# Attention scores from one full pass and one pass of half the rows, with two blocks of keys side by side

## The chip, the cores and the metric

The kernel runs on one core of a Trainium2 chip. The metric is the device time of one execution in microseconds (us); lower is better. The engines are named as the profile names them: PE is the matrix engine, PEld its loads of the stationary operand, DVE, ACT and POOL the vector, scalar and general engines, and SP the queue that issues most transfers.

## What is computed

The reference, cut to its three parts, with 8 batches of 3072 rows, 256 columns and 64 score dimensions:

```
scores = matmul(z, z.T) / S                  # per batch, z is 3072 x 64
x = u * matmul(maximum(scores, 0) ** 2, v)   # attention without a softmax
x = x / sqrt(mean(x * x) + 1e-6) * rms_g     # norm over the 256 columns
x = (silu(x @ w_gate) * (x @ w_val)) @ w_out
out = for each row: the expert with the largest x @ r_gate, relu(x @ w1[e]) @ w2[e], times two gates
```

All is kept close to float32 by cutting each operand into a high and a low part of the type float32r and summing the products high by high, high by low and low by high.

## The kernel before

**Tiling.** A batch's 3072 rows are 6 groups of 512 queries, J counts these 48 groups, and 24 blocks of 128 keys, taken two at a time. So a group has 12 steps, counted by `kp`, and there are 576 such steps of attention (class `Attn`). 18 steps behind them (`AHEAD`) runs the gated layer of the group (class `Glu`), 12 steps of its own per group, one for each 128 of the 1536 hidden columns. The function `pair` writes one step of each, interleaved by hand; the order on each engine is the order of writing. The experts follow when both are done.

**Operands of the scores.** `z_job` transposes 512 rows of z into a tile `p`: partitions 0 to 63 hold the high part of z transposed (64 dimensions), partitions 64 to 127 the low part, for every block of keys. The low part is DVE's line L441, the high part ACT's line L450. `make_q` copies `p` of the group's own 512 queries with the halves exchanged into a tile `q`, by two ACT instructions (L468, L471) that stand two steps apart. In `Attn.first` each block of keys takes two passes over 512 queries with the same stationary slice of `p`: L504 streams `p` (high by high plus low by low), L505 streams `q` (high by low plus low by high), and both sum in one PSUM bank `s`. ACT's L507 reads the bank (relu and scale), L512 squares, L515 rounds to the high part `ha`, DVE's L521 makes the low part `la`, and one step later L535 to L537 multiply them by v, 24 passes of 256 columns.

**Order of PE in a step.** Scores of this step (4 passes of 512), gate and value products of the gated layer (L648, 12 passes of 512), products with v of the step before (24 of 256), output product of the gated layer of the step before (L673 to L675, 6 of 512). PSUM has four banks for scores and gate products together (pool `sc`), handed out in turn.

**Around a group.** `load_u` fetches the group's u (512 KB) in the middle of the group, at `kp` 6; the tile has one buffer. `Attn.leave` multiplies the sums by u into a tile `x`, squares it on ACT into u's tile for the norm's sums (L552), scales x (L568) and turns it by 16 DVE blocks into `xf` (L599). These stand in `side`, a planner that gives out queued work step by step and is forced (`side.until`) where a result is needed. `split_x` then rounds `xf` on ACT (L628) and DVE (L629) to `xTh` and `xTl`, on which the next group's first L648 waits. `f32t("sg")` has two buffers, for the gate products `sg`. SP works in order; each of its transfers is written behind those that were written before it.

**Parts of the array's rows.** An operand of up to 32 or up to 64 partitions is set by the built program on a quarter or a half of the array's 128 rows. Before, only four instructions are: the transposes of a 12-row table (L894) in the first of two calls of `table`; those of the second call have 91 rows and stand on all 128.

Of the kernel before, what the change touches and what calls it, by code (L numbers as in the profile page):

```python
# [8 lines left out]
F32 = mybir.dt.float32  # L9
F32R = mybir.dt.float32r  # L10
# [3 lines left out]
AF = mybir.ActivationFunctionType  # L14
ALU = mybir.AluOpType
# [10 lines left out]
def attention_glu_routed(ctx: ExitStack, tc: tile.TileContext, u, v, z, w_gate, w_val, w_out, rms_g, r_gate, r_og, w1, w2, out):  # L26
# [12 lines left out]
    nc = tc.nc  # L39
    B, S, D = u.shape  # L40
    DQ = z.shape[2]
    FF = w_gate.shape[1]
    E, _, F2 = w1.shape
# [23 lines left out]
    sc = ctx.enter_context(tc.tile_pool(name="sc", bufs=4, space=PSUM))  # L67
# [7 lines left out]
    def bank(pool, name):  # L75
        return pool.tile([128, 512], F32, tag="sc" if pool is sc else "acc", name=name)
# [3 lines left out]
    def f32t(tag, name):  # L80
        return st.tile([128, 512], F32, tag=tag, name=name, bufs=BUFS.get(tag, 2))
# [318 lines left out]

    vt, pt, qt = {}, {}, {}
    z_chain = Chain()

    def v_job(b, kp, tag):
        t = {}
# [15 lines left out]
    def z_job(b, c, tag):  # L421
        t = {}

        def load():
            t["r"] = f32t(tag, "z_raw")
            nc.sync.dma_start(
                out=t["r"][:, 0:256].rearrange("p (a d) -> p a d", a=4), in_=z[b, c * 512 : (c + 1) * 512, :].rearrange("(a p) d -> p a d", p=128)
            )

        def work():  # L430
            z_chain.end()
            zf = bank(sc, "zT")
            for i in range(2):
                nc.tensor.transpose(zf[:, i * 128 : (i + 1) * 128], t["r"][:, i * 128 : (i + 1) * 128], ident)
            x = at.tile([128, 512], F32R, tag="p", name="p", bufs=NC)
            xv = x.rearrange("p (i k c) -> p i k c", i=2, k=2)
            zv = zf[:, 0:256].rearrange("p (i c) -> p i c", i=2)

            def low():
                for k in range(2):  # L440
                    nc.vector.tensor_tensor(  # L441
                        out=xv[64:128, :, k], in0=zv[64 * k : 64 * k + 64], in1=xv[0:64, :, k].bitcast(F32), op=ALU.subtract
                    )
                pt[b, c] = x
                if c == 0:
                    make_q(b * NC)

            def high():
                for k in range(2):
                    nc.scalar.activation(out=xv[0:64, :, k], in_=zv[64 * k : 64 * k + 64], func=AF.Copy)  # L450

            z_chain.begin(high, low)

        return load, 0.6, work, tag, 3.9 if b else 0.0
# [8 lines left out]

    def make_q(J):
        b, c = divmod(J, NC)
        q = at.tile([128, 512], F32R, tag="q", name="q")
        p = pt[b, c]
        nc.scalar.activation(out=q[0:64], in_=p[64:128].bitcast(F32), func=AF.Copy)  # L468

        def other():  # L470
            nc.scalar.activation(out=q[64:128], in_=p[0:64].bitcast(F32), func=AF.Copy)  # L471
            qt[J] = q

        if J:
            side.after(2, other)
        else:
            other()


    xt, xf, ut = {}, {}, {}  # L480
    squared, turned = set(), set()

    def load_u(J):
        b, c = divmod(J, NC)
# [3 lines left out]
    class Attn:  # L488
# [7 lines left out]
        def first(self):  # L496
            b = self.b
            ahead = min(NC - 1, (self.kp + 2) // 2)
            side.until(lambda: (b, ahead) in pt and self.J in qt and (b, 2 * max(0, self.kp - 1)) in vt, -1)
            for j in range(2):  # L500
                kb = 2 * self.kp + j
                ps = bank(sc, "s")
                w = pt[b, kb // 4][:, (kb % 4) * 128 : (kb % 4 + 1) * 128]
                nc.tensor.matmul(ps, lhsT=w, rhs=pt[b, self.c], start=True, stop=False)  # L504
                nc.tensor.matmul(ps, lhsT=w, rhs=qt[self.J], start=False, stop=True)  # L505
                r = f32t("r", "r")
                nc.scalar.activation(out=r, in_=ps, func=AF.Relu, scale=SCALE)  # L507
                self.r.append(r)
# [30 lines left out]
        def leave(self):  # L539
            J = self.J  # L540
            side.until(lambda: J == 0 or J - 1 in turned, 0)
            x, uu = at.tile([128, 4, D], F32, tag="x", name="x", bufs=1), ut.pop(J)
            xt[J] = x
            for k in range(2):
                v4 = lambda t: t[:, 2 * k : 2 * k + 2]
                nc.vector.tensor_tensor(out=v4(x), in0=self.accs[k].rearrange("p (a c) -> p a c", a=2), in1=v4(uu), op=ALU.mult)
            ss, y, tmp = small([128, 4], "ss"), small([128, 4], "yi", I32), small([128, 4], "nt")
            yf = y.bitcast(F32)

            def squares(k):  # L550
                for qb in (2 * k, 2 * k + 1):
                    nc.scalar.activation(out=uu[:, qb], in_=x[:, qb], func=AF.Square, accum_out=ss[:, qb : qb + 1])  # L552
                if k:
                    squared.add(J)

            def root():

                nc.vector.tensor_scalar(out=ss, in0=ss, scalar1=1.0 / D, scalar2=1e-6, op0=ALU.mult, op1=ALU.add)
                nc.vector.tensor_scalar(out=y, in0=ss.bitcast(I32), scalar1=-0.5, scalar2=1597463007.0, op0=ALU.mult, op1=ALU.add)
                for _ in range(3):  # L560
                    nc.gpsimd.tensor_tensor(out=tmp, in0=yf, in1=yf, op=ALU.mult)
                    nc.gpsimd.tensor_tensor(out=tmp, in0=tmp, in1=ss, op=ALU.mult)
                    nc.gpsimd.tensor_scalar(out=tmp, in0=tmp, scalar1=-0.5, scalar2=1.5, op0=ALU.mult, op1=ALU.add)
                    nc.gpsimd.tensor_tensor(out=yf, in0=yf, in1=tmp, op=ALU.mult)

            def scale(k):
                for qb in (2 * k, 2 * k + 1):
                    nc.scalar.activation(out=x[:, qb], in_=x[:, qb], func=AF.Copy, scale=yf[:, qb : qb + 1])  # L568

            side.add(1.0, None, 0)  # L570
            side.add(0.1, lambda: squares(0), 0)
            side.add(0.1, lambda: squares(1), 0)
            side.add(3.0, None, 0)
            side.add(0.4, root, 0)
            side.add(6.0, None, 0)
            side.add(0.1, lambda: scale(0), 0)
            side.add(0.1, lambda: scale(1), 0)
            side.add(2.0, None, 0)
            turn_x(J)
# [497 lines left out]
    def pair(n, m):  # L1077

        a = g = None
        if n is not None:  # L1080
            J, kp = divmod(n, NP)
            a = Attn(J, kp, lists.setdefault(("a", J), []))
            a.first()
        if m is not None:
            J, f = divmod(m, NF)
            side.until(lambda: J in xT, 0)
            g = Glu(J, f, lists.setdefault(("g", J), []))
            g.first()
        pa, pg = last["a"], last["g"]
        last["a"], last["g"] = a, g  # L1090
        for step in (pa, pg):
            if step:
                step.second()
        if a:
            a.high(0, nc.scalar if g else nc.vector)
        t = Turn()
        t.time = (3.75 if a else 0.0) + (4.19 if g else 0.0)
        t.budget = 4.0 if a and g else 1.5 if a else 1.9
        side.tick(t)
        if a:  # L1100
            a.low(0)
        if g:
            g.gate()
            g.product()
            if g.f == NF - 1 and g.J + 1 < NJ - 1:
                side.until(lambda: g.J + 1 in turned, 0)
                split_x(g.J + 1)
        if a:
            a.high(1, nc.scalar if g else nc.vector)
            a.low(1)  # L1110
        if g:
            g.part()
            g.rest()
        if pa and pa.kp == NP - 1:
            pa.leave()
        if pg and pg.f == NF - 1 and pg.J < NJ - 1:
            pg.leave()
        if a:

            if a.kp == NP // 2 and a.J:  # L1120
                side.until(lambda: a.J - 1 in squared, 0)
                load_u(a.J)
            if a.kp == NP // 2 and a.c < NC - 1:
                make_q(a.J + 1)
            if a.c == NC - 1 and a.b + 1 < B:
                if a.kp % 2:
                    side.jobs([z_job(a.b + 1, a.kp // 2, "raw")])
                if a.kp:
                    side.jobs([v_job(a.b + 1, a.kp - 1, "raw")])
            if a.c == 0 and a.b and a.kp == 0:  # L1130
                side.jobs([v_job(a.b, NP - 1, "raw")])
            if a.J >= 2 and a.kp in (NP // 2, NP - 1):
                spare(1)
# [98 lines left out]
```

## Time and profile before

| | us |
|---|---|
| median of 3 runs | 6101.07 (6096.69 to 6106.18) |
| the profiled execution | 6110.35 |
| its span, first to last instruction | 6108.6 |
| PE busy | 5868.4 (96%) |
| DVE busy | 4141.2 (68%) |
| ACT busy | 3418.4 (56%) |
| mean granted clock of PE | 0.983 |

A row of a timeline gives start and duration in us, engine, line, operation, the tile written and the tiles read; brackets give the idle time before it and what ended it. The ends of matmuls are modelled and overlap the next start, so the pace of PE is read from start to start. A PEld row is the load of the stationary slice for the matmul of the same line; in a steady stream it starts together with the matmul before.

### The profile page before, as it was taken

Reading aid. Unit: us, or ns where it says so; the run is one execution under the profiler, and the core shown is the slowest. Engines: PE = TensorE matmul, PEld = TensorE weight load, DVE = VectorE, ACT = ScalarE, POOL = GpSimd, SP = SyncE. Lnnn points to the kernel's source line nnn. Section 1 sums busy time; section 2 is a strip of 40 time slices with the busy share of each in tenths; the row PEclk is TensorE's granted clock in tenths of the full one; section 3 lists DMA queues with packets and bytes.
Section 4 is the critical chain, followed back from the end, with each engine's and each line's share of the span. In section 5 each row is a group of like instructions: output and inputs, shape, how many; then the busy total and the mean of one; then the engine's idle time right before and its main releaser. Section 6 shows DMA issues by size and latency. Waiting matters only on the chain. (4 is left out here: it accounts for less than half of the span.)

```text
span 6108.6 us, 95345 instructions
## 1 busy us (share of the span) xinstructions
PE 5868.4 (96%) x35032; PEld 5155.5 (84%) x35032; DVE 4141.2 (68%) x8920; ACT 3418.4 (56%) x6610; POOL 1151.3 (19%) x1729
## 2 busy tenths in 40 slices
PE   6899999999999999999999999999999889999998
PEld 5688888888888888888888888888888779999998
DVE  6666666665666566666666666657565678888886
ACT  4566666666666666666666666666666423333332
POOL 2212101210121012101211030103000023333333
PEclk8999999999999999999999999999999999999999
DMA  2101100110010001001110010001000112232241
GB/s 70 47 25 49 34 25 30 46 34 23 30 49 30 23 30 49 30 27 32 47 32 22 29 32 13 15 12 36 8 15 8 47 55 101 101 103 101 102 139 57
DMA packets 199592, 268.27 MB, mean 44 GB/s; under 512 B 46988, under 2 KB 176016, under 8 KB 190928
## 3 DMA queue, kind: packets, MB, share of 16 engines
q1 hardware_dynamic: 173664, 210.29, 10.7%
q0 software_dynamic: 25456, 51.83, 2.7%
q8 instruction: 278, 4.55, 0.3%
q14 instruction: 194, 1.59, 0.1%
HBM read 528.71 MB, written 86.71 MB: 101 GB/s over the span
## 5 line engine op out<-in xcount | busy, mean ns | idle before, releaser
L537 PE MATMUL o<-v,la 128*128 128x256 f32 x4608 | 1298.3, 282 | 29.3 <-DVE la L521 29.2
L535 PE MATMUL o<-v,ha 128*128 128x256 f32 x4608 | 1291.9, 280 | 5.3 <-DVE ha L517 5.2
L536 PE MATMUL o<-v,ha 128*128 128x256 f32 x4608 | 1291.2, 280 | 0.0
L521 DVE TENSOR_TENSOR la<-r,ha 128x512 fp32r<-128x512 f32 x1152 | 835.9, 726 | 663.5 <-ACT ha L515 658.0
L507 ACT ACTIVATE r<-s 128x512 f32<-128x512 f32 x1152 | 624.8, 593 | 859.4 <-PE s L505 806.5
L648 PE MATMUL g<-xTh,wg 128*128 128x512 f32 x2304 | 844.7, 408 | 131.9 <-ACT xTh L628 102.7
L656 DVE TENSOR_TENSOR sg<-g,sg 128x512 f32<-128x512 f32 x1152 | 793.9, 689 | 196.0 <-ACT sg L652 133.5
L537 PEld LDWEIGHTS o<-v,la 128*128 128x128 f32 x4608 | 871.5, 189 | 33.2 <-DVE la L521 32.9
L535 PEld LDWEIGHTS o<-v,ha 128*128 128x128 f32 x4608 | 872.6, 189 | 29.5 <-DVE ha L517 6.4
L536 PEld LDWEIGHTS o<-v,ha 128*128 128x128 f32 x4608 | 871.9, 189 | 25.6
L648 PE MATMUL g<-xTh,wv 128*128 128x512 f32 x2304 | 831.2, 402 | 5.7 <-ACT wv L93 3.0
L515 ACT ACTIVATE ha<-r 128x512 fp32r<-128x512 f32 x1116 | 705.7, 632 | 38.6
L512 ACT ACTIVATE r<-r 128x512 f32<-128x512 f32 x1152 | 721.7, 627 | 1.0
L648 PEld LDWEIGHTS g<-xTh,wg 128*128 128x128 f32 x2304 | 443.2, 192 | 263.7 <-ACT xTh L628 122.9
L1007 PE MATMUL h<-gh,W 128*128 128x256 f32 x3200 | 641.2, 283 | 5.4 <-ACT gh L93 4.1
L660 ACT ACTIVATE hg<-sg 128x512 fp32r<-128x512 f32 x576 | 363.6, 631 | 487.2 <-DVE sg L656 431.3
L1026 PE MATMUL eo<-W,hx 128*128 128x512 f32 x1600 | 580.2, 395 | 0.7 <-DVE o L1039 0.7
L1007 PEld LDWEIGHTS h<-gh,W 128*128 128x128 f32 x3200 | 526.9, 191 | 25.3 <-ACT gh L93 5.5
L648 PEld LDWEIGHTS g<-xTh,wv 128*128 128x128 f32 x2304 | 446.1, 194 | 109.9 <-PE g L648 3.8
L599 DVE STREAM_TRANSPOSE gTf<-xg 32x128 f32<-32x128 f32 x1600 | 483.3, 302 | 49.2 <-DMA xg<-xs,clip 26.9
L1010 ACT ACTIVATE hx<-h 128x512 fp32r<-128x512 f32 x400 | 236.7, 595 | 496.0 <-PE h L1007 493.5
L96 POOL TENSOR_TENSOR le<-e_raw,he 128x512 fp32r<-128x512 f32 x64 | 83.0, 1297 | 2119.9 <-ACT he L93 2119.9
(170 smaller groups left out, 11046.8 us busy)
## 6 DMA issues: line engine op xcount, KB each, us to landing
W<-ws SPq DMA_DIRECT2D x400, 1024.0 KB
v_raw<-in_v SPq DMA_DIRECT2D x96, 256.0 KB
u<-in_u SPq DMA_DIRECT2D x48, 512.0 KB
xs<-rec SPq DMA_DIRECT2D x48, 512.0 KB
e_raw<-in_moe_w SPq DMA_DIRECT2D x64, 256.0 KB
ws<-he SPq DMA_DIRECT2D x64, 256.0 KB
ws<-le SPq DMA_DIRECT2D x64, 256.0 KB
z_raw<-in_z SPq DMA_DIRECT2D x48, 128.0 KB
```

The lines of the kernel that those rows point to most:

```text
L507: nc.scalar.activation(out=r, in_=ps, func=AF.Relu, scale=SCALE)
L512: nc.scalar.activation(out=r, in_=r, func=AF.Square)
L515: nc.scalar.activation(out=self.ab[j][0], in_=r, func=AF.Copy)
L521: nc.vector.tensor_tensor(out=l, in0=self.r[j], in1=h.bitcast(F32), op=ALU.subtract)
L535: nc.tensor.matmul(o, lhsT=ah[:, cs], rhs=vh, start=kb == 0 and qb % 2 == 0, stop=False, skip_group_check=True)
L536: nc.tensor.matmul(o, lhsT=ah[:, cs], rhs=vl, start=False, stop=False, skip_group_check=True)
L537: nc.tensor.matmul(o, lhsT=al[:, cs], rhs=vh, start=False, stop=kb == NK - 1, skip_group_check=True)
L599: nc.vector.transpose(out=ov[32 * q : 32 * q + 32, :, :, i, :], in_=iv[32 * i : 32 * i + 32, :, :, q, :])
L648: nc.tensor.matmul(ps, lhsT=a[:, d, fs], rhs=x[:, d], start=n == 0, stop=n == 5)
L656: nc.vector.tensor_tensor(out=self.sg, in0=ps, in1=self.sg, op=ALU.mult)
L1007: nc.tensor.matmul(o, lhsT=w[:, c0 : c0 + 128], rhs=x[:, d], start=n == 0, stop=n == 5)
L1026: nc.tensor.matmul(self.accs[t], lhsT=h[:, cs], rhs=w, start=f == 0, stop=False)
```

## The change

Three things are changed.

First, the scores. `p` now holds, for even blocks of keys, the high part in partitions 0 to 63 and the low part in 64 to 127, and for odd blocks the other way round. There are two query tiles: `q0` has the high part in both halves, `q1` the low part in both. A step first streams `q0` through all 128 rows for both blocks (L503: high by high plus low by high), then streams one half of `q1` for each block through that half of the rows that holds the keys' high part (L506: high by low), rows 0 to 63 for the even block and 64 to 127 for the odd one. The product low by low is no longer computed. Both PSUM banks of a step are taken ahead of the first matmul, and the two relu instructions stand behind all four matmuls.

Second, `make_q` is eight transfers inside SBUF on SP (64 partitions by 2 by 128 numbers each) in place of two ACT instructions.

Third, to pay for the second query tile, the tile `x` is gone: u is overwritten by the norm's input, the squares go to a buffer of `sg`, and `load_u` of a group waits until the group before is turned, where it waited for its squares.

```
@@ z_job: low and high
-                        out=xv[64:128, :, k], in0=zv[64 * k : 64 * k + 64], in1=xv[0:64, :, k].bitcast(F32), op=ALU.subtract
+                    here, there = half[k], half[1 - k]
+                    nc.vector.tensor_tensor(out=xv[there, :, k], in0=zv[here], in1=xv[here, :, k].bitcast(F32), op=ALU.subtract)
-                    nc.scalar.activation(out=xv[0:64, :, k], in_=zv[64 * k : 64 * k + 64], func=AF.Copy)
+                    nc.scalar.activation(out=xv[half[k], :, k], in_=zv[half[k]], func=AF.Copy)
@@ make_q
-        q = at.tile([128, 512], F32R, tag="q", name="q")
-        nc.scalar.activation(out=q[0:64], in_=p[64:128].bitcast(F32), func=AF.Copy)
...
-            nc.scalar.activation(out=q[64:128], in_=p[0:64].bitcast(F32), func=AF.Copy)
+        qs = [at.tile([128, 512], F32R, tag=f"q{k}", name=f"q{k}") for k in range(2)]
+        for part in range(2):
+            for k in range(2):
+                for to in half:
+                    nc.sync.dma_start(out=view(qs[part])[to, :, k].bitcast(F32), in_=view(pt[b, c])[half[k ^ part], :, k].bitcast(F32))
@@ Attn.first
-            for j in range(2):
-                kb = 2 * self.kp + j
-                ps = bank(sc, "s")
-                w = pt[b, kb // 4][:, (kb % 4) * 128 : (kb % 4 + 1) * 128]
-                nc.tensor.matmul(ps, lhsT=w, rhs=pt[b, self.c], start=True, stop=False)
-                nc.tensor.matmul(ps, lhsT=w, rhs=qt[self.J], start=False, stop=True)
+            pss = [bank(sc, "s") for _ in kbs]
+            for ps, w in zip(pss, ws):
+                nc.tensor.matmul(ps, lhsT=w, rhs=qh, start=True, stop=False)
+            for ps, w, h in zip(pss, ws, half):
+                nc.tensor.matmul(ps, lhsT=w[h], rhs=ql[h], start=False, stop=True)
+            for ps in pss:
                 r = f32t("r", "r")
                 nc.scalar.activation(out=r, in_=ps, func=AF.Relu, scale=SCALE)
@@ Attn.leave
-            x, uu = at.tile([128, 4, D], F32, tag="x", name="x", bufs=1), ut.pop(J)
+            x = xt[J] = ut.pop(J)
-                    nc.scalar.activation(out=uu[:, qb], in_=x[:, qb], func=AF.Square, accum_out=ss[:, qb : qb + 1])
+                t = f32t("sg", "xx")
+                    nc.scalar.activation(out=t[:, i * D : (i + 1) * D], in_=x[:, qb], func=AF.Square, accum_out=ss[:, qb : qb + 1])
@@ pair
-                side.until(lambda: a.J - 1 in squared, 0)
+                side.until(lambda: a.J - 1 in turned, 0)
                 load_u(a.J)
```

On PE, in a step of attention with the gated layer beside it, the rows stood so before; `y` is the output product of the step before, `s` the scores (tiles `p` and `q`), `g` the gate products:

```order
L675 MATMUL y_5768<-hg_6372,wo1_99 128x512
L504 MATMUL s_6492<-p_5371,p_5572 128x512
L505 MATMUL s_6492<-q_5565,p_5572 128x512
L504 MATMUL s_6497<-p_5371,p_5572 128x512
L505 MATMUL s_6497<-q_5565,p_5572 128x512
L648 MATMUL g_6502<-xTh_5601,wg0_94 128x512
L648 MATMUL g_6502<-xTl_5602,wg0_94 128x512
```

and now:

```order
L676 MATMUL y_5823<-hg_6043,wo1_99 128x512
L503 MATMUL s_6135<-q0_4668,p_402 128x512
L503 MATMUL s_6136<-q0_4668,p_402 128x512
L506 MATMUL s_6135<-q1_4669,p_402 128x512
L506 MATMUL s_6136<-q1_4669,p_402 128x512
L649 MATMUL g_6145<-xTh_5656,wg0_94 128x512
L649 MATMUL g_6145<-xTl_5657,wg0_94 128x512
```

The row that streamed `q` behind each block's first pass is gone; the two full passes follow each other, and the two half passes (64 of 128 rows each, which the names do not show) follow them, ahead of the gate products, whose order is unchanged.

On SP, in the middle of a group, with `rec` the rows that the gated layer stores, `e_raw`, `he` and `le` an expert's weights on their way, the transfers stood so before:

```order
L386 DMA ws<-he 128x2x256
L386 DMA ws<-le 128x2x256
L784 DMA xs<-rec 128x4x256
L486 DMA u<-in_u 128x4x256
L377 DMA e_raw<-in_moe_w 128x2x256
L386 DMA ws<-he 128x2x256
L386 DMA ws<-le 128x2x256
```

and now:

```order
L386 DMA ws<-he 128x2x256
L386 DMA ws<-le 128x2x256
L785 DMA xs<-rec 128x4x256
L483 DMA u<-in_u 128x4x256
L473 DMA q_15400<-p 64x2x128 x4
L473 DMA q_15401<-p 64x2x128 x4
L377 DMA e_raw<-in_moe_w 128x2x256
L386 DMA ws<-he 128x2x256
L386 DMA ws<-le 128x2x256
```

The eight transfers of `q0` and `q1` stand right behind that of u, so whatever holds the transfer of u holds them too, and the loads of weights stand eight transfers later.

Also on SP, at the program's very start, where `z_raw` and `v_raw` are the first blocks of z and v, the transfers stood so before:

```order
L426 DMA z_raw<-in_z 128x4x64 x2
L409 DMA v_raw<-in_v 128x2x256 x2
L426 DMA z_raw<-in_z 128x4x64
L486 DMA u<-in_u 128x4x256
L409 DMA v_raw<-in_v 128x2x256 x2
L426 DMA z_raw<-in_z 128x4x64
```

and now:

```order
L427 DMA z_raw<-in_z 128x4x64 x2
L410 DMA v_raw<-in_v 128x2x256 x2
L427 DMA z_raw<-in_z 128x4x64
L473 DMA q_124<-p 64x2x128 x4
L473 DMA q_125<-p 64x2x128 x4
L483 DMA u<-in_u 128x4x256
L410 DMA v_raw<-in_v 128x2x256 x2
L427 DMA z_raw<-in_z 128x4x64
```

The eight transfers of the first group's query tiles now stand ahead of u and of the next blocks of v and z.

## Rows read from the trace of the kernel before

**Rows 1.** The page's first part: busy time, share, instructions of each engine.
```profile
PE 5868.4 (96%) x35032; PEld 5155.5 (84%) x35032; DVE 4141.2 (68%) x8920; ACT 3418.4 (56%) x6610; POOL 1151.3 (19%) x1729
```

**Rows 2.** Stretches: from:to, length; PE, PEld, DVE, ACT, POOL busy; clock, DMA share, GB/s.
```profile
0.00:136.00 136.00, 85.95 (x496) 75.71 (x496) 91.56 (x186) 58.84 (x122) 40.60 (x70) 0.87 0.24 70
136.00:4686.00 4550.00, 4419.22 (x25400) 3828.47 (x25401) 2937.35 (x5806) 2901.59 (x5570) 673.55 (x1214) 0.99 0.10 30
```

**Rows 3.** Timeline of PE, one step's scores and their neighbours.
```profile
3001.65 0.40 PE L504 MATMUL s<-p 128*128 128x512 f32 x1
3001.88 0.39 PE L505 MATMUL s<-q,p 128*128 128x512 f32 x1
3002.11 0.39 PE L504 MATMUL s<-p 128*128 128x512 f32 x1
3002.33 0.39 PE L505 MATMUL s<-q,p 128*128 128x512 f32 x1
3002.56 0.40 PE L648 MATMUL g<-xTh,wg 128*128 128x512 f32 x1
```

**Rows 4.** Waits of PE: tile, line, releaser; us in total, times, longest.
```profile
PE g L648 <- ACT xTh L628: 102.7, 47, 11.1
PE o L537 <- DVE la L521: 29.2, 15, 4.8
...
PE o L535 <- DVE ha L517: 5.2, 1, 5.2
PE s L504 <- DVE sg L656: 4.4, 6, 0.8
```

**Rows 5.** Timeline of PE at one group's first gate product.
```profile
2976.08 0.50 PE L648 MATMUL g<-xTh,wg 128*128 128x512 f32 x1 [3.12 <-ACT xTh L628]
```

**Rows 6.** The stretch soon after it, in the columns of rows 2.
```profile
2977.87:2981.28 3.41, 3.08 (x8) 1.92 (x7) 1.98 (x3) 3.34 (x8) 0.00 (x0) 0.50 0.02 6
```

**Rows 7.** Timeline of PE and PEld where 12-row transposes give way to full passes.
```profile
4885.56 0.26 PE L894 MATMUL ids<-ident,plain 12*128 12x12 f32 x1
4885.75 0.29 PEld L648 LDWEIGHTS g<-xTh,wg 128*128 128x128 f32 x1
...
4885.91 0.33 PEld L648 LDWEIGHTS g<-xTl,wg 128*128 128x128 f32 x1
...
4886.34 0.63 PE L648 MATMUL g<-xTl,wg 128*128 128x512 f32 x1
...
4886.77 0.63 PE L648 MATMUL g<-xTh,wg 128*128 128x512 f32 x1
```

**Rows 8.** The same where 91-row transposes give way to full passes.
```profile
5052.31 0.24 PE L894 MATMUL ids<-ident,plain 91*128 91x91 f32 x1
...
5052.32 0.19 PEld L1026 LDWEIGHTS eo<-W,hx 128*128 128x128 f32 x1
...
5052.43 0.19 PEld L1027 LDWEIGHTS eo<-W,lx 128*128 128x128 f32 x1
```

**Rows 9.** Timeline of PEld where a weight load had to wait.
```profile
4870.40 0.19 PEld L674 LDWEIGHTS y<-lg,wo 128*128 128x128 f32 x1 [0.29 <-DVE lg L663]
...
4870.51 0.19 PEld L675 LDWEIGHTS y<-hg,wo 128*128 128x128 f32 x1
```

**Rows 10.** The costliest groups and two tiles' views: ACT and the transfer of u.
```profile
L507 ACT ACTIVATE r<-s 128x512 f32<-128x512 f32 x1152 | 624.8, 593 | 859.4 <-PE s L505 806.5
...
L471 ACT ACTIVATE q<-p x48: 628/630/632, 6.3 to 4689.6; 64x512 fp32r<-64x512 f32 x48
...
L486 SPq DMA_DIRECT2D u<-in_u x48: 417/459/2099, 3.4 to 4752.8; - x48
```

**Rows 11.** Waits of the SP queue, in the columns of rows 4.
```profile
SPq L784 <- DVE rec L615: 1508.9, 40, 98.5
```

**Rows 12.** Timeline of the start: first transfers and who waits for them.
```profile
0.81 1.00 SPq L426 DMA_DIRECT2D z_raw<-in_z  x2
...
3.24 0.66 PE L434 MATMUL zT<-ident,z_raw 128*128 128x128 f32 x2 [3.24 <-DMA z_raw<-in_z]
```

More of the change, by code (lines that the diff above doesn't have):

```diff
@@ L402, in attention_glu_routed @@
     z_chain = Chain()
+    half = (slice(0, 64), slice(64, 128))
     def v_job(b, kp, tag):
@@ L440, in low @@
                 for k in range(2):
-                    nc.vector.tensor_tensor(
-                        out=xv[64:128, :, k], in0=zv[64 * k : 64 * k + 64], in1=xv[0:64, :, k].bitcast(F32), op=ALU.subtract
-                    )
+                    here, there = half[k], half[1 - k]
+                    nc.vector.tensor_tensor(out=xv[there, :, k], in0=zv[here], in1=xv[here, :, k].bitcast(F32), op=ALU.subtract)
                 pt[b, c] = x
@@ L465, in make_q @@
         b, c = divmod(J, NC)
-        q = at.tile([128, 512], F32R, tag="q", name="q")
-        p = pt[b, c]
-        nc.scalar.activation(out=q[0:64], in_=p[64:128].bitcast(F32), func=AF.Copy)
-        def other():
-            nc.scalar.activation(out=q[64:128], in_=p[0:64].bitcast(F32), func=AF.Copy)
[L472 to L477, printed above, removed]
+        qs = [at.tile([128, 512], F32R, tag=f"q{k}", name=f"q{k}") for k in range(2)]
+        view = lambda t: t.rearrange("p (i k c) -> p i k c", i=2, k=2)
+        for part in range(2):
+            for k in range(2):
+                for to in half:
+                    nc.sync.dma_start(out=view(qs[part])[to, :, k].bitcast(F32), in_=view(pt[b, c])[half[k ^ part], :, k].bitcast(F32))
+        qt[J] = qs
     xt, xf, ut = {}, {}, {}
-    squared, turned = set(), set()
+    turned = set()
     def load_u(J):
@@ L499, in first @@
             side.until(lambda: (b, ahead) in pt and self.J in qt and (b, 2 * max(0, self.kp - 1)) in vt, -1)
-            for j in range(2):
-                kb = 2 * self.kp + j
-                ps = bank(sc, "s")
-                w = pt[b, kb // 4][:, (kb % 4) * 128 : (kb % 4 + 1) * 128]
-                nc.tensor.matmul(ps, lhsT=w, rhs=pt[b, self.c], start=True, stop=False)
-                nc.tensor.matmul(ps, lhsT=w, rhs=qt[self.J], start=False, stop=True)
+            qh, ql = qt[self.J]
+            kbs = (2 * self.kp, 2 * self.kp + 1)
+            ws = [pt[b, kb // 4][:, (kb % 4) * 128 : (kb % 4 + 1) * 128] for kb in kbs]
+            pss = [bank(sc, "s") for _ in kbs]
[4 more added lines that the diff above has]
+            for ps in pss:
                 r = f32t("r", "r")
@@ L541, in leave @@
             side.until(lambda: J == 0 or J - 1 in turned, 0)
-            x, uu = at.tile([128, 4, D], F32, tag="x", name="x", bufs=1), ut.pop(J)
-            xt[J] = x
+            x = xt[J] = ut.pop(J)
             for k in range(2):
                 v4 = lambda t: t[:, 2 * k : 2 * k + 2]
-                nc.vector.tensor_tensor(out=v4(x), in0=self.accs[k].rearrange("p (a c) -> p a c", a=2), in1=v4(uu), op=ALU.mult)
+                nc.vector.tensor_tensor(out=v4(x), in0=self.accs[k].rearrange("p (a c) -> p a c", a=2), in1=v4(x), op=ALU.mult)
             ss, y, tmp = small([128, 4], "ss"), small([128, 4], "yi", I32), small([128, 4], "nt")
@@ L550, in squares @@
             def squares(k):
-                for qb in (2 * k, 2 * k + 1):
-                    nc.scalar.activation(out=uu[:, qb], in_=x[:, qb], func=AF.Square, accum_out=ss[:, qb : qb + 1])
-                if k:
-                    squared.add(J)
+                t = f32t("sg", "xx")
+                for i, qb in enumerate((2 * k, 2 * k + 1)):
+                    nc.scalar.activation(out=t[:, i * D : (i + 1) * D], in_=x[:, qb], func=AF.Square, accum_out=ss[:, qb : qb + 1])
             def root():
```

## The prediction, made before the change was run

> **What bounds the kernel now.** I read the shares first: PE is busy 96% of the span, DVE 68%, ACT 56% [rows 1]. By stretches, up to 136 us, before the gated layer starts, PE is busy 86 of 136 us and runs behind the others; from 136 to 4686 us, where attention and the gated layer run together, it is busy 4419 of 4550 us [rows 2]. So in that second stretch a step takes as long as its work on PE. The timeline of one step gives the pace: the four score passes and the first gate pass start at 3001.65, 3001.88, 3002.11, 3002.33 and 3002.56 [rows 3], 0.23 us from start to start. The waits of PE show what else there is: 102.7 us in 47 pieces, 2.2 us each, at a group's first gate product, for ACT's `xTh` [rows 4]; one is shown, 3.12 us long [rows 5]. Soon behind it stands a stretch of 3.41 us at half the granted clock (1.2 GHz) [rows 6]. The mean clock of 0.99 in the whole stretch [rows 2] says that such half-clock time costs some 1% of 4550, about 45 us. What counts for the change is thus PE's own time per step, less what a stall swallows.
>
> **The pass that goes.** Four passes of 512 columns become two, plus two half passes that use different rows of the array. If these two run side by side, the step loses one pass: -0.23 us [rows 3].
>
> **The two changes of rows.** Each step now goes from 128 rows to 64 and back. The trace shows one such change, at L894: transposes on 32 rows give way to full passes. The last of them starts at 4885.56, the next weight load at 4885.75, and the load behind it, which in a steady stream starts with the first one's matmul, at 4885.91 [rows 7]. Where the transposes have 91 rows and thus stand on all 128, the last starts at 5052.31 and the next weight load at 5052.32 [rows 8]. So across a change the weight load isn't fetched ahead: it stood 0.19 us, as if the matmul before had to be out of the array, and then its own 0.16 us lay bare. All this at half clock, since the passes behind it are 0.43 apart (4886.34, 4886.77 [rows 7]). At full clock a bare load costs 0.11 us (4870.40 to 4870.51 [rows 9]), that is 0.66 of 0.16. The standing time was measured behind 12 columns, which take next to nothing to stream; behind 512 columns it is added to their 0.23. At full clock it is between half (0.09, if it goes with the clock) and all of 0.19; I take 0.12, the ratio of the bare loads. A change then takes 0.23 + 0.12 + 0.11 = 0.46 from start to start where 0.23 stood, an extra of 0.23; bounds 0.20 and 0.30. Entering the half rows isn't in the trace, so its extra alone is bounded by 0, if its weights can be fetched ahead, and 0.30; I take the value of leaving, the nearest row. Two changes: +0.46 (0.40 to 0.60 if both are alike).
>
> The Trainium skill (TensorEngine Tiling (Array Packing), Key Properties) says that changing the tiling mode, not just the tile, drains the engine. The row shows it for leaving; by that rule entering pays as well. With the latency and the load time of its page TensorE: Matmul & The Clock Gate (Single matmul latency; LDWEIGHTS), 0.38 and 0.11 us for 512 columns, an estimate for a change is an extra of 0.26, and the sum below would be 31 us longer. No run here shows those two figures.
>
> **The second half pass.** Its weights go to other rows. Between 0, if they load beside the first half's, and 0.11, a bare load [rows 9], it starts behind the first; 0.23, a pass, if the halves don't overlap at all. I take 0.05, since the load is behind another in one queue but doesn't meet its rows.
>
> So a step: -0.23 + 0.46 + 0.05 = **+0.28 us**; from 0.40 - 0.23 = 0.17 to 0.60 - 0.23 + 0.11 = 0.48.
>
> **How many steps pay.** Of 576 steps, 18 run ahead of the gated layer, where PE isn't the bound [rows 2]; 47 more stand ahead of a stalled gate product, and the stall swallows their 0.28 [rows 4]. 576 - 18 - 47 = 511 steps by 0.28: **+143 us**. Shorter stalls should also give back some half-clock time: between 0 and the 45 us; I take **-10 us**.
>
> **The query tiles by DMA.** At the start the eight transfers stand ahead of the next loads. SP takes 0.5 us to issue one (two in 1.00), and a load issued by 1.3 us is used at 3.24, some 2 us [rows 12]; so 8 x 0.5 + 2 in place of two ACT copies of 0.63 [rows 10]: **+5 us**, once (0 to 10). Later the tiles are written in the middle of a group, six steps or some 49 us (4550 / 558 = 8.2 a step [rows 2]) ahead of use, behind the transfer of u; nothing ever waited for u, which stands at the same place (48 transfers [rows 10], and no row of PE's or DVE's waits names it). The 96 copies leave ACT, 60 us, but ACT waits 806.5 us for the scores [rows 10], so it brings nothing.
>
> **Edits at nothing.** The relu now starts when all four matmuls are done, some 0.5 us later; behind it stand square, rounding and DVE's low part, needed a step later. PE waited for `ha` once and for `la` 15 times in the run [rows 4]; if that cover were gone, 558 x 0.5 = 279 us would be the price. Both score banks are taken at once: so far PE waited 4.4 us for one [rows 4], at worst some more of that kind. The squares in a buffer of `sg` put a wait for DVE's low part ahead of ACT's next sigmoid, at most 0.7 us in 48 places, 34 us, hidden by ACT's waiting for PE. The later transfer of u waits for DVE's turning; `split_x` is forced by the same result a step earlier, so SP stands for a few us at most, and u has half a group to land.
>
> **Sum.** 143 - 10 + 5 = +138 on the profiled execution's 6110, which is 9 us above the median of 6101: 6248 there, and **6239 us** for the median. With the bounds of a step (511 x 0.17 = 87, 511 x 0.48 = 245) and those of the small terms (-45 to 0, 0 to 10): 6143 to 6356.
>
> **Rivals.** *Faster: a change of rows costs nothing, and the halves overlap.* Then a step loses 0.23 - 0 to 0.11, and 511 steps give -61 to -118 us, with the +5 about 5990 to 6045. For it speaks that weight loads are fetched ahead everywhere else in the stream [rows 3, 8]; against it the one change that the trace has [rows 7]. It decides where two extras and the offset stay under 0.23: under 0.09 to 0.11 for a change, less than the bare load and the standing time together at any clock shown. The skill's page TensorE: Matmul & The Clock Gate (Part 3) lets tiles of different rows start about 4 ns apart, which is the overlap of this case; no run here shows it.
>
> *Half the price: only leaving the half rows costs.* The row is of leaving alone. A step: 0.23 + 0.05 - 0.23 = +0.05, from -0.03 to +0.18; 511 steps, with +5: 6091 to 6196, most likely 6132.
>
> *The halves don't overlap.* Then nothing is saved and the changes are paid: 0.46 a step (to 0.60), +235 to +307 with +5: 6341 to 6413. Nothing in the trace shows two matmuls side by side.
>
> *The query tiles come late.* SP has stood up to 98.5 us at the store ahead of them [rows 11]; it had nothing else to issue, but were one late by 5 us in each of 42 groups, it would cost 210 us: about 6450.
>
> **Chances.** Both changes paid, 0.57; half the price, 0.16; faster, 0.14; no overlap, 0.10; late tiles, 0.03. A measurement of this kernel tells about 0.2%, 12 us, from no change. Faster by more takes the 0.14 and 0.03 of the half price; within, 0.05; slower, 0.78. The range leaves out the faster case, the late tiles and the end of the no-overlap case: 6085 to 6390.
>
> **What would show it.** From the second L503 to the first L506, and from the second L506 to the first L649, start to start: 0.46 says paid, 0.23 says free. The two L506 0 to 0.11 apart: side by side; 0.23: not. L506's weight load starting with the matmul before it would refute the standing time. The idle time at a group's first gate product should be shorter by 0.3. A wait of PE for a DMA into `q0` or `q1` behind the first group, or more waits for `la`, would show a cost that I set at nothing. A step shorter than before would make the forecast wrong in sign.

## The result, and the profile after

| | before | after |
|---|---|---|
| median, both measured together (us) | 6099.25 (4 runs) | 6186.93 (6186.07 to 6189.24, 4 runs) |
| ratio | | 1.0143 [1.0125, 1.0160] |
| PE busy in the profiled execution | 5868.4 | 5957.1 |
| mean granted clock | 0.983 | 0.982 |

The change makes the kernel slower by 88 us. The forecast was 6239, in the range 6085 to 6390: the sign and the mechanism were right, the cost of a step was forecast too large, what the stalls swallow too small, and a term set at nothing was not nothing. In what follows, the first row is the page's first part of after, in the order of [rows 1]; the second is the core's span and clock.

```profile
PE 5957.1 (96%) x35032; PEld 5015.3 (81%) x35032; DVE 4149.8 (67%) x8920; ACT 3359.1 (54%) x6514; POOL 1155.8 (19%) x1729
```
```profile
core 0: 6184.4 us, clock 0.982
```

PE has as many instructions as before, 35032, and is busy 89 us longer, while ACT is busy 59 us less: the 96 copies are gone, and no gain from it shows in the time. Where PE's time goes is seen in one step of after, all of PE's rows from its first score pass to the gate products, with the weight loads (PEld) that stand with them; "x2" is two instructions in one row:

```profile
3008.25 0.62 PE L503 MATMUL s<-q,p 128*128 128x512 f32 x2
3008.80 0.19 PEld L506 LDWEIGHTS s<-q,p 64*128 64x128 f32 x2 [0.36 <-issue]
3008.80 0.50 PE L506 MATMUL s<-q,p 64*128 64x512 f32 x2
3009.23 0.19 PEld L649 LDWEIGHTS g<-xTh,wg 128*128 128x128 f32 x1 [0.24 <-issue]
3009.23 0.50 PE L649 MATMUL g<-xTh,wg 128*128 128x512 f32 x1
...
3009.56 0.40 PE L649 MATMUL g<-xTl,wg 128*128 128x512 f32 x1
...
3009.80 0.40 PE L649 MATMUL g<-xTh,wg 128*128 128x512 f32 x1
```

Three things are to be seen, against [rows 3]. The two half passes share one row of 0.50 us, no longer than the single L649 below them: they run side by side. The load for the half passes begins at 3008.80, together with its own matmul, and behind a gap that the profile calls "issue", since nothing that it shows was waited for; in a steady stream a load begins with the matmul before. The same stands in front of L649. So both changes of rows, into the half rows and out of them, stop the stream.

Over the 558 steps that have the gated layer beside them, the median distances between starts, from the first score pass to the second gate product, are in us (worked out from all rows of that kind in each trace):

| | to the 2nd | 3rd | 4th | first gate | second gate | sum |
|---|---|---|---|---|---|---|
| before | 0.232 | 0.227 | 0.227 | 0.227 | 0.237 | 1.150 |
| after | 0.230 | 0.326 | 0.003 | 0.430 | 0.334 | 1.323 |

A step costs 0.173 more. A matmul's row begins with its own weight load where that lies bare. So the 0.326 is a pass of 0.23 and a standing time of 0.09; the 0.430 is a bare load of 0.11, a half pass of 0.23 and 0.09 again; the 0.334 is a bare load of 0.11 and a pass. Each change costs 0.09 + 0.11 = 0.20 extra, entering and leaving alike, and the second half pass costs 0.003. Thus -0.23 + 0.40 + 0.00 = +0.17.

The waits of PE after (tile, line, releaser; us in total, times, longest), against [rows 4]:

```profile
PE g L649 <- ACT xTh L629: 92.7, 47, 11.1
...
PE o L539 <- DVE la L523: 22.7, 12, 3.3
...
PE s L503 <- DVE sg L657: 4.1, 6, 1.0
PE g L649 <- DVE lgs L728: 3.9, 7, 0.6
...
PE s L503 <- DMA q<-p: 3.6, 1, 3.6
...
PE s L506 <- DMA q<-p: 0.9, 1, 0.9
```

The wait for `xTh` went from 102.7 to 92.7, as often as before. PE waited twice for a query tile, 4.5 us in all, at the start and nowhere else: its first score passes come at 8.41 and 10.46.

```profile
8.41 1.19 PE L503 MATMUL s<-q,p 128*128 128x512 f32 x2 [3.64 <-DMA q<-p]
10.46 1.48 PE L506 MATMUL s<-q,p 64*128 64x512 f32 x2 [0.86 <-DMA q<-p]
```

### The profile page after: what moved, and what is told of

The parts are those of the page before. It is cut to its first block, busy times and chain, and to the rows that moved or that the text cites. A ratio compares the mean times of both kernels' runs of the same rounds, so it can differ in the third digit from the quotient of the medians.

```text
span 6184.4 us, 96127 instructions
## 1 busy us (share of the span) xinstructions
PE 5957.1 (96%) x35032; PEld 5015.3 (81%) x35032; DVE 4149.8 (67%) x8920; ACT 3359.1 (54%) x6514; POOL 1155.8 (19%) x1729
## 5 line engine op out<-in xcount | busy, mean ns | idle before, releaser
L649 PE MATMUL g<-xTh,wg 128*128 128x512 f32 x2304 | 888.8, 427 | 127.4 <-ACT xTh L629 92.7
L649 PE MATMUL g<-xTh,wv 128*128 128x512 f32 x2304 | 835.1, 403 | 6.3 <-ACT wv L93 3.0
L649 PEld LDWEIGHTS g<-xTh,wg 128*128 128x128 f32 x2304 | 440.0, 191 | 343.2 <-ACT xTh L629 107.9
L649 PEld LDWEIGHTS g<-xTh,wv 128*128 128x128 f32 x2304 | 446.8, 194 | 113.3 <-PE g L649 4.8
```

Source lines behind the costliest of these rows:

```text
L649: nc.tensor.matmul(ps, lhsT=a[:, d, fs], rhs=x[:, d], start=n == 0, stop=n == 5)
```

## The experiments

All ratios are to the kernel before as it was measured beside the run, with a 95% interval, and a kernel's "excess" is its median less that median of before (6099.25 for after, 6103.25 for e1 to e4, 6101.72 for e5 to e8, 6098.36 for e9 and e10), so that kernels measured at different times can be set side by side; that of after is +88. The intervals make an excess uncertain by 6 to 10 us. Distances in a step are medians as above; "idle" is 4550 us less PE's busy time in the stretch from 136 to 4686 us (before 130.8, after 127.8), and "half-clock time" is the part of that stretch in which the clock's records in the trace show half of the full clock (before 121, after 124); about half of such time is lost. Where a cost of a step is multiplied over the run, the count is 532, which is fitted to the last experiment and not counted.

**e1: is it the half passes?** The changed kernel with the second passes over all 128 rows:

```
-            for ps, w, h in zip(pss, ws, half):
-                nc.tensor.matmul(ps, lhsT=w[h], rhs=ql[h], start=False, stop=True)
+            for ps, w in zip(pss, ws):
+                nc.tensor.matmul(ps, lhsT=w, rhs=ql, start=False, stop=True)
```

> The second pass of each block streams q1 through all 128 rows, so the product low by low comes back and no matmul of the scores uses half the rows; the transfers for the query tiles and the norm in u's place stay. Theory (the changes of rows cost all that was lost): the score part of a step takes 0.92 us again, and the time is that of the kernel before plus 3 to 5 us at the start: 6102 to 6105. Rival (the transfers or the norm's buffers carry a part of the 88 us): above 6115.

Measured: 6125.53, ratio 1.0032 [1.0020, 1.0043], excess +22; a step takes 1.150, as before. So 65 of the 88 us hang on the half passes, and 22 lie in the other parts, which the theory had put at nothing but the start. Waits of PE:

```profile
PE g L647 <- ACT xTh L627: 108.4, 48, 11.1
...
PE g L647 <- DVE lgs L726: 3.7, 7, 0.5
PE g L647 <- DVE p L443: 3.6, 5, 0.7
```

The wait for `lgs` at a gate product is not there before, and that for `p` was 1.8 us; but both are a few us only; idle is 144.1 (busy 4405.95) and half-clock time 137.

**e2: do the halves overlap in the changed kernel?** Both halves on rows 0 to 63; the high part is put there for every block:

```
...
-            for ps, w, h in zip(pss, ws, half):
+            for ps, w, h in zip(pss, ws, (half[0], half[0])):
```

> The high part of every block lies in partitions 0 to 63 again, so both half passes of a step use rows 0 to 63. The trace after shows 0.43 us from the first half pass to the next gate product, which has two readings. Theory (the halves run side by side, and 0.43 is a bare weight load of 0.11, one pass of 0.23 and a standing time of 0.09): the halves now run one behind the other, 0.66 in place of 0.43, 511 x 0.23 = +118, about 6305. Rival (the halves already run one behind the other, 0.215 each, and leaving the half rows costs only a bare load): no difference, about 6187.

Measured: 6244.68, ratio 1.0231 [1.0214, 1.0248], excess +141; a step takes 1.548, 0.225 more than after, one pass. PE in a step:

```profile
3009.79 0.62 PE L502 MATMUL s<-q,p 128*128 128x512 f32 x2
...
3010.34 0.29 PEld L505 LDWEIGHTS s<-q,p 64*128 64x128 f32 x2 [0.36 <-issue]
3010.34 0.73 PE L505 MATMUL s<-q,p 64*128 64x512 f32 x2
...
3011.00 0.50 PE L648 MATMUL g<-xTh,wg 128*128 128x512 f32 x1
```

The two L505 take 0.73 together, where after's L506 take 0.50. So the overlap is real and worth a whole pass. But the time grew by 54 us only (141 less 88), where 532 x 0.225 is 120. The rest is in the stalls:

```profile
PE g L648 <- ACT xTh L628: 60.8, 47, 11.1
```
```profile
136.00:4686.00 4550.00, 4466.11 (x24673) 3628.85 (x24674) 2866.11 (x5649) 2762.90 (x5328) 667.62 (x1197) 0.99 0.12 35
```

Idle falls from 127.8 to 83.9, 44 us, and half-clock time from 124 to 82, worth half of that, 21: 120 - 44 - 21 = 55, beside 54 measured. A longer step on PE shortens the wait for `xTh` at the group's end, and the half-clock stretch behind it.

**e3: half the changes for the same work.** The four half passes of two steps stand together in every second step; in the other steps there are none, so that their blocks miss high by low, and the blocks of every second step have it twice:

```
+            n = 0 if self.kp % 2 else 2
...
+            for i in range(n):
+                for ps, w, h in zip(pss, ws, half):
+                    nc.tensor.matmul(ps, lhsT=w[h], rhs=ql[h], start=False, stop=i == n - 1)
```

> The half passes of two steps are done together in every second step, four in a row, two by two in different rows; in the other step there are none, so rows are changed half as often. The step with four adds its own halves twice and the other leaves high by low out; the number of passes is that of the change. Theory (the price goes with the number of changes, 0.20 each, and halves overlap): two steps take 0.40 - 0.46 = -0.06 against before, 511 x -0.03 = -15 and +4 at the start: about 6088. Rival (halves run one behind the other, entering costs 0.10 and leaving 0.11): four halves take 0.86, two steps 1.99 in place of 1.84, 511 x 0.075 = +38 and +4: about 6141.

Measured: 6124.30, ratio 1.0036 [1.0022, 1.0051], excess +21. Two steps take 1.555 + 0.696 = 2.251, against 2.300 before: two changes paid once, two passes saved, -0.46 + 0.40 = -0.06 by the terms, -0.05 measured. In the time, 266 x 0.05 = 13 us should be seen against e1, and 1 is. Half-clock time is 187 here against e1's 137, 25 us dearer, which would more than eat it; the core's mean clock is lower too. With idle 3 us longer (147.1) the three make +15 where -1 was measured, so this sum doesn't come out. That and the reason for more half-clock time are left open.

```profile
core 0: 6122.6 us, clock 0.978
```

**e4: four changes a step.** One loop, so that full and half passes alternate:

```
-            for ps, w in zip(pss, ws):
+            for ps, w, h in zip(pss, ws, half):
                 nc.tensor.matmul(ps, lhsT=w, rhs=qh, start=True, stop=False)
-            for ps, w, h in zip(pss, ws, half):
                 nc.tensor.matmul(ps, lhsT=w[h], rhs=ql[h], start=False, stop=True)
```

> Full pass and half pass of the even block, then full pass and half pass of the odd block: four changes of rows in a step in place of two, and no two halves side by side. Theory (0.20 a change, halves overlapped before): 4 x 0.20 and no pass saved, +0.80 a step against before, 511 x 0.80 = +409: about 6505. Rival (halves never overlapped; entering 0.10, leaving 0.11): 2 x 0.21 and 4 passes, +0.42 less the 0.03 by which a half is shorter, 511 x 0.39 = +200: about 6300.

Measured: 6406.83, ratio 1.0499 [1.0481, 1.0516], excess +304. PE in a step:

```profile
3016.49 0.40 PE L502 MATMUL s<-q,p 128*128 128x512 f32 x1
...
3016.81 0.50 PE L503 MATMUL s<-q,p 64*128 64x512 f32 x1
...
3017.24 0.50 PE L502 MATMUL s<-q,p 128*128 128x512 f32 x1
...
3017.67 0.50 PE L503 MATMUL s<-q,p 64*128 64x512 f32 x1
...
3018.10 0.50 PE L646 MATMUL g<-xTh,wg 128*128 128x512 f32 x1
...
3018.44 0.39 PE L646 MATMUL g<-xTl,wg 128*128 128x512 f32 x1
```

The first distance, into half rows, is 0.32: a pass and a standing time. The next three are 0.43, bare load, pass and standing time, behind half and full passes alike, and the last, 0.34, is a bare load and a pass. The step takes 1.957, +0.807, which is four times 0.20. This sum alone doesn't tell entering from leaving, since e4 doubles both; the rows do. If entering were free, the first distance would be 0.23, and no load would lie bare at a half pass; that rival falls. The time again grew by less, since the stalls gave back:

```profile
PE g L646 <- ACT xTh L626: 30.6, 9, 11.1
```

Against e1, 532 x 0.807 = 429; idle falls from 144.1 to 38.8 and half-clock time from 137 to 67, 105 and 35 us: 289, beside 281 measured (304 less 22).

**e5: how much does a shorter step bring?** No half passes at all; the product high by low is left out.

```
-                nc.tensor.matmul(ps, lhsT=w, rhs=qh, start=True, stop=False)
-            for ps, w, h in zip(pss, ws, half):
-                nc.tensor.matmul(ps, lhsT=w[h], rhs=ql[h], start=False, stop=True)
+                nc.tensor.matmul(ps, lhsT=w, rhs=qh, start=True, stop=True)
```

> The change without its half passes: two full passes in a step, high by low left out. No change of rows is left. A step should lose 0.45 us against four full passes (1.15 to 0.70). Theory (what a step gains or loses on PE is partly given back by the stalls for xTh and by half-clock time, by a third to a half, as in the runs with longer steps): 6125 - 490 x 0.45 x 0.5 to 0.7 = 5970 to 6015. Rival (every step that isn't stalled counts fully): about 5905.

Measured: 6002.59, ratio 0.9835 [0.9820, 0.9850], excess -99; a step takes 0.696, two passes less than e1, 532 x 0.454 = 242, yet only 121 us come out (99 and 22). By idle (230.6) and half-clock time (254) 87 and 59 us go, which would leave 96; the other 25 stay open. The wait for `xTh` is the longest of all kernels:

```profile
PE g L645 <- ACT xTh L625: 186.8, 48, 11.6
```

So the stalls work both ways: roughly a third to a half of what PE's step gains or loses goes into them and the half-clock time.

**e6 and e7: the 22 us of the other parts.** e6 is e1 written block by block (bank, both passes, relu); the transfers and the norm in u stay. e7 is the kernel before, with only the order changed: both banks, both passes with `p`, both with `q`, then the relus.

```
e6 against e1
-            pss = [bank(sc, "s") for _ in kbs]
-            for ps, w in zip(pss, ws):
+            for w in ws:
+                ps = bank(sc, "s")
...
e7 against before
-            for j in range(2):
-                ps = bank(sc, "s")
...
+            pss = [bank(sc, "s") for _ in kbs]
+            for ps, w in zip(pss, ws):
...
+            for ps, w in zip(pss, ws):
...
+            for ps in pss:
```

> The kernel of the run with four full passes, written block by block again: bank, q0, q1, relu, then the same for the odd block. The transfers for the query tiles and the norm in u's place stay. That run was 22 us above before with the same 1.15 us a step, its extra in 15 more stalled steps at the first gate products. Theory (taking both banks at once and starting the first relu later carries it): 6102 to 6108. Rival (the transfers or the norm's buffers carry it): about 6125.

> The kernel before with nothing changed but the order inside a step: both banks first, p through both blocks, then q through both blocks, then both relu instructions; query tiles by ACT, x in a tile of its own. Theory (the order carries the 22 us): 6118 to 6125. Rival (the transfers or the norm's buffers do): about 6103.

Measured: e6 6108.91, ratio 1.0010 [1.0001, 1.0019], excess +7; e7 6124.84, ratio 1.0038 [1.0024, 1.0052], excess +23. A step takes 1.150 in both. So the order carries 15 us taken out of e1 (22 to 7) and 23 put into before, and the transfers with the norm in u some 7. Among the waits of e7 the new one for `lgs` shows, and little else:

```profile
PE g L650 <- ACT xTh L630: 105.6, 47, 11.1
...
PE g L650 <- DVE lgs L729: 3.8, 7, 0.5
```

Idle is 138.4 in e7 against 130.8 before, and 144.1 in e1 against 134.2 in e6; half-clock time is 137 in e1 against 127 in e6. For the pair e1 and e6 that is 10 + 5, the 15 us; for e7 it is 8 of the 23, and its half-clock time is 151 where before has 121, half of which difference is the other 15. That the relu 0.5 us later passes on to the group's end, where `xTh` is late, fits these rows, but no run tells it apart from taking both banks at once, and none shows why there is more half-clock time; this is left open.

**e8: the order of the two kinds of passes.** Half passes first, then the full ones:

```
+            for ps, w, h in zip(pss, ws, half):
+                nc.tensor.matmul(ps, lhsT=w[h], rhs=ql[h], start=True, stop=False)
             for ps, w in zip(pss, ws):
-                nc.tensor.matmul(ps, lhsT=w, rhs=qh, start=True, stop=False)
-            for ps, w, h in zip(pss, ws, half):
-                nc.tensor.matmul(ps, lhsT=w[h], rhs=ql[h], start=False, stop=True)
+                nc.tensor.matmul(ps, lhsT=w, rhs=qh, start=False, stop=True)
```

> The change with the two half passes ahead of the two full ones: as many changes of rows, but the even block's bank is complete one pass (0.23 us) before the odd one's. Theory (a change costs the same in either order, and an earlier first relu shortens some stalls): 6172 to 6187, with 1.32 us from the first pass to the second gate product as in the change. Rival (the price hangs on which pass follows the half ones): a step differs by 0.05 us or more, 25 us or more either way.

Measured: 6171.44, ratio 1.0111 [1.0096, 1.0127], excess +70, 18 us less than the change. The price of a step is the same: counted from the last output product, 1.55 against 1.56; from the first pass it is 1.23 and not the 1.32 expected, since the standing time now lies ahead of that pass. What gains is the wait, which is shorter though no work of ACT or DVE was added or removed:

```profile
PE g L647 <- ACT xTh L627: 83.0, 47, 11.0
```

Idle is 113.3 against 127.8, and half-clock time hardly differs (122 against 124). What in the order shortens it was not tried.

**e9: the stall itself.** In all these kernels the wait for `xTh` gives or takes. It hangs on the planner: ahead of the squares of the norm, `Attn.leave` puts an entry of 1.0 without work into the planner's queue, a pause. The kernel before without that line:

```
-            side.add(1.0, None, 0)
             side.add(0.1, lambda: squares(0), 0)
```

> The kernel before with one entry of the planner's queue gone, the wait of 1.0 ahead of the norm's squares: each later piece of the norm then falls one step earlier, and the 16 turning blocks no longer stand as 11 ahead of and 5 behind the gated layer's products in the group's last step, but 9 a step earlier and 7 ahead of them. Theory (PE's waits for xTh and the half-clock time behind them, which give back part of what a longer step costs, come from these blocks standing in DVE's way): the 80 us of such waits from 300 us on fall to under 40, with some of the half-clock time: 6030 to 6070. Rival (PE would wait for ACT's xTh whatever DVE does): 6095 to 6105.

Measured: 5951.98, ratio 0.9758 [0.9744, 0.9771], excess -146: more than expected, and the fastest kernel of this study. The rows that answer to [rows 4] and to [rows 2], and ACT's wait for DVE's `xf` ahead of `xTh`, before and in e9:

```profile
PE o L537 <- DVE la L521: 28.3, 14, 6.0
...
PE g L647 <- ACT xTh L627: 19.3, 3, 10.1
```
```profile
136.00:4686.00 4550.00, 4506.91 (x26266) 3938.78 (x26267) 3024.48 (x6006) 2999.08 (x5747) 647.73 (x1244) 1.00 0.10 30
```
```profile
ACT xTh L628 <- DVE xf L599: 316.9, 48, 9.1
```
```profile
ACT xTh L627 <- DVE xf L598: 23.4, 12, 10.0
```

44 of the 47 stalls are gone, idle falls from 130.8 to 43.1, and the clock goes from 0.99 to 1.00. ACT's wait for DVE's turned blocks falls from 316.9 to 23.4, so these blocks were what made `xTh` late. These rows show 88 of the 146 us as idle time. Half-clock time is 39 where before has 121: half of the difference is 41. The other 17 stay open.

**e10: the change without the stall.** e8 with the same line removed:

> The change with its half passes first and the same entry of the planner gone. Theory (the price of a step is 0.17, and where fewer stalls are left to swallow it, it is paid in full): the run without that wait and with full passes plus 85 to 95 us. Rival (the give-back has nothing to do with the stalls for xTh): plus 60 to 65 us, as between the two kernels that keep the entry (6171 and 6109).

Measured: 6044.04, ratio 0.9911 [0.9895, 0.9926], excess -54.

```profile
PE g L646 <- ACT xTh L626: 18.8, 2, 10.0
```

It is 92 us behind e9. With hardly a stall left to swallow anything, the 92 us are 92 / 0.173 = 532 steps' worth, nearly all 558. The pair differs in the transfers, the norm in u and the order as well: idle is 49.1 against 43.1 and half-clock time 41 against 39, so some 7 of the 92 us are not PE's step. The best kernel is the one before with the planner's line gone; the change costs there what its step costs.

## Why the prediction was right, and where its sizes were off

**The account of the 88 us.** By the excesses, after less e1 is 65, the half passes; e1 less e6 is 15, the order of banks, passes and relu; e6 itself is 7, the transfers and the norm in u. Such differences add up to the whole by construction; what speaks for the parts is that e7 puts 23 into before by the order alone. The half passes cost 92 where nothing swallows them; of this, idle gives back 16 (144.1 to 127.8) and half-clock time 7 (half of 137 less 124), which leaves 69 beside the 65 measured.

**The pass that goes, -0.23.** Right: e2, without the overlap, is longer by 0.225.

**The two changes of rows, +0.46.** Right in kind, +0.40 in size, the low bound. The standing time was scaled from a half-clock row of 0.19 [rows 7] by the ratio of the bare loads, 0.66, to 0.12; it is 0.09. The scaling held, the row did not carry over. One step of after runs at half clock (0.50 in the second row):

```profile
111.79 1.05 PE L503 MATMUL s<-q,p 128*128 128x512 f32 x2
...
112.78 0.52 PE L506 MATMUL s<-q,p 64*128 64x512 f32 x2
```
```profile
111.79:112.78 0.99, 0.99 (x4) 0.34 (x4) 0.40 (x2) 0.43 (x2) 0.53 (x1) 0.50 0.72 222
```

Two passes of 0.43 leave 0.13 of the 0.99 for the standing time, and 0.66 of that is the 0.09. Leaving 64 rows costs the same 0.13 at half clock in e8, where 0.72 lies between a pair of half passes and the next full pass (48.76 to 49.48 us): 0.16, 0.43 and 0.13. The row of 0.19 was of 32 rows and 12 columns, and no run tells which of the two makes it longer. The bare load of 0.11 [rows 9] was right, and that row shows it, though the prediction says that no run does. Taking entering for as dear as leaving, though the trace had only leaving, was the choice that decided, and e4's rows bear it out. The rule that the prediction drew from the Trainium skill (TensorEngine Tiling (Array Packing), Key Properties), that a change of the tiling mode drains the engine, agrees with this trace in both directions, 0.20 each. The estimate of 0.26 from the Trainium skill's page TensorE: Matmul & The Clock Gate (Single matmul latency; LDWEIGHTS) was too much; measurement decides for 0.20.

**The second half pass, +0.05.** It was 0.003: the load does go beside the first one's. Where both halves meet the same rows, in e2, the second costs a whole pass. The Trainium skill's 4 ns (TensorE: Matmul & The Clock Gate, Part 3) agree with these 3.

So the step is +0.17 and not +0.28; times 511 that is 87 in place of 143, and this is the larger part of the miss.

**How many steps pay, 511.** This step failed. The stalls were taken to swallow 0.28 once in each of 47 places. They swallow more: twelve steps make PE 2.1 us slower in a group, and the wait for `xTh` comes out 0.33 shorter in each (108.4 in e1 to 92.7), idle time by 16 us in all, and half-clock time goes with it. With the stalls, 65 / 0.173 = 376 steps' worth came out; nearly without them (e10 against e9), 532. The half-clock time, -10 by the forecast, did not shrink against before (121 to 124), since the order of writing added as much as the longer step took away; against e1 it did, worth 7 us. Its bound of 45 was read from the rounded clock of 0.99; 121 us at half clock cost some 60.

That the forecast's sum would come to 87 - 10 + 5 = 82 with the right price of a step, close to the 88, is luck: the stalls and the half-clock time took away 22 of the 87 where 10 was forecast, and the order with the transfers brought 22 where 5 was.

**The start, +5.** The two waits for a query tile make 4.5 us, and all of e6, which has the norm in u as well, 7; the bound of 10 held. That tiles come late elsewhere is refuted: PE waited for none behind the first group.

**Edits at nothing.** That the 96 ACT copies bring nothing fits: e6, which is without them, is still 7 us slower than before; their share was not run by itself. That taking both banks at once and the later relu cost nothing is wrong: 15 to 23 us (e6, e7). PE's wait for a score bank was watched, and it stayed: 4.1 us, where [rows 4] have 4.4; the cost showed in longer stalls and more half-clock time, which the prediction had not tied to the order.

**The signs named ahead.** The first to be read, 0.46 from start to start, was put badly: a matmul's row begins with its own bare load, so a change spreads over two distances, 0.33 and 0.43 and then 0.33. Summed over both changes it is 0.40 over three passes of 0.23. Two L506 0 to 0.11 apart: seen, 0.003. The load of L506 starting with the matmul before, which would have refuted the standing time: not seen. A shorter idle at the group's first gate product: seen, 0.2 per piece (102.7 to 92.7 in 47). More waits for `la`: not seen, 12 against 15.

**Rivals.** Changes that cost nothing: refuted, 0.20 each, twice the point from which that case decides (0.09 to 0.11). Half the price: refuted by the bare load of the half passes and by e4's rows; its upper bound should read 6198, 0.18 x 511 + 5 above the median, and not 6196. Halves that don't overlap: refuted by e2. Late query tiles: refuted by the waits (40 groups have theirs made in the middle of a group, not 42).

## What to carry to other kernels

Count the changes between parts of the array and the whole before counting the columns saved: a pair of half passes saves 0.23 us here, a way in and out costs 0.40, so at least two pairs have to share one way. That shortens the step (e3, by 0.05 in two), but e3's time, 6124, was no better than e1's 6126. When the bounding engine also stalls once a group for another, a step's price counts only in part, some half to seven tenths here, and the first thing to look for is what makes the stall: one planned pause was worth 146 us, more than the whole price of the half passes. An edit of order that leaves an engine's own step unchanged, as in e7, can still cost 0.4%, here seen as more idle and half-clock time.

## What the runs showed of the hardware

Unexpected were four things. Loads and matmuls of two halves of the rows start 3 ns apart, though they are issued one behind the other. Entering half rows costs as much as leaving them, though no row of before showed it. The standing time is 0.13 at half clock and 0.09 at full, so it shrinks by the ratio of the bare loads (0.16 to 0.11) and doesn't halve. And behind a half pass on the same rows the next load is fetched ahead as usual: in e2 both loads of the half passes are done in 0.29, while the second half pass starts 0.335 behind the first, which is the first one's bare load of 0.11 and one pass; only a change between half and all rows stopped it in these runs.
